# Value products in quarters: riding in the free row tiles of score steps

## The chip, the cores and the metric

The kernel runs on one core of one Trainium2 chip. What counts is the device time of one execution in microseconds (us). The kernel before takes 698.33 us in the median of 3 runs (698.25 to 699.32); the execution that the hardware profiler recorded took 699.02 us, of which 697.3 us lie between its first and its last instruction (the span).

## The reference

Two independent layers over 2048 positions of 640 channels; their outputs stand side by side.

```python
# A: a diagonal state space layer, P = 640 complex states
Lam_bar = exp(dt * Lam);  B_bar = ((Lam_bar - 1) / Lam)[:, None] * Bmat
Bu = einsum("bld,pd->blp", x, B_bar)
h[t] = Lam_bar * h[t-1] + Bu[t]                      # 2048 steps
y = 2 * einsum("blp,dp->bld", h, Cmat).real + x * Dskip
# B: attention, 32 heads of 20, ONE key head and ONE value head for all
q = x @ wq;  k = x @ wk (640 -> 20);  v = x @ wv (640 -> 20)
p = softmax(einsum("bhqd,bkd->bhqk", q, k) * 20**-0.5)
b = einsum("bhqk,bkd->bhqd", p, v) -> (2048, 640) @ wo
```

Inputs and output are bf16. The attention has 32 heads x 2048 x 2048 scores, and their exponentials are most of the work.

## The kernel before

**Tiles.** A score tile is 128 keys x 512 queries of one head. There are 2048 of them (`NTILE`): 4 query blocks x 8 groups of 4 heads x 16 key chunks x 4 heads. 64 successive tiles (4 heads, 16 key chunks) make a block; there are 32 blocks.

**Scores (row tiles).** A score product contracts 20 channels and one row for a bias, so it needs 32 of the 128 rows of TensorE's array. Keys and queries are held four times, at partitions 0, 32, 64 and 96, and up to four products of 32 rows x 128 columns (`tile_position` (32j, 0)) run side by side in one *score step*. `fill` makes a step: two or three tiles for ScalarE, and up to two for VectorE. The results stand in two slots of three PSUM banks, `SC0` and `SC1`; one exp is read out of the one while TensorE fills the other.

**Exponentials.** ScalarE takes two or three tiles in one ACTIVATE (line 1540) and writes bf16 to `PR`. VectorE takes the other tiles: it makes an int16 of a score whose bits are about those of the exponential in bf16 (line 875, to the buffer `BIG`), and shifted copies of it, which GpSimd (line 1913) and VectorE make, correct it in the mean. Each tile of VectorE's so has four value products, on scaled values `VS`, and each of ScalarE's has one, on plain values `VP`.

**Value products (column tiles).** A value product contracts 128 keys to 20 values and a sum, and fills 32 columns of the array. `pv_source` gathers one product of each of the four heads of a block and `pv` issues them as one *column step*, side by side (`tile_position` (0, 32j)), 512 queries each; line 2012. All add up in one PSUM bank, `MB3` (`pvbank`), head j in partitions 32j to 32j + 31. A step may have fewer than four where buffers run short or where the block's products run out. When a block has all its products VectorE copies the bank out (`pvsb`), and the next block's begin.

**The rest of the products** (projections, output projection, state space layer) are written as steps in column tiles too, four quarters of the output columns side by side (`ride` and `product`, line 808). `board` lets such a product *ride*: cut along the contraction into four pieces of 32 rows (`piece`, line 818), each takes a row tile of a score step that the scores leave free. One product at a time may be open, and pieces that found no place are issued alone.

**Order.** All order is made before the launch, by a list scheduler (`Schedule`) with costs of its own: each engine takes the ready instruction with the least priority number, and semaphores follow from the order. `STAGES` holds the rules (priorities, shares, limits) by the number of the score tile reached: SHARE is the part of the tiles that VectorE takes, EV the priority of copies out of PSUM, PV that of value products, BACKLOG and ROOM2 how many copies and free buffers are kept, AHEAD and EARLIER which block VectorE's tiles come from. `background` lists when the other products are due, in score tiles (`CB_FROM`, `Y_STEP`). Engines execute in order and wait for semaphores.

## Time and profile before

| | |
|---|---|
| median of 3 runs | 698.33 us |
| the profiled execution, its span | 699.02 us, 697.3 us |
| TensorE: matmuls, instructions | 683.8 us (98% of the span), 11489 |
| ScalarE | 683.9 us (98%), 705 |
| VectorE | 615.0 us (88%), 1135 |
| GpSimd | 473.1 us (68%), 602 |
| DMA | 34.46 MB, mean 49 GB/s |
| granted TensorE clock | 1.000 |

A matmul's record begins when its data start to stream and ends when its last result is modelled to land, and a record of ScalarE's reaches past the start of the next one. So a busy share near 100% says that an engine was in use, not that it could not have done more: for both, the distance from one start to the next has to be read.

### The profile page before, as it was taken

Reading aid. Unit: us, or ns where it says so; the run is one execution under the profiler, and the core shown is the slowest. Engines: PE = TensorE matmul, PEld = TensorE weight load, DVE = VectorE, ACT = ScalarE, POOL = GpSimd, SP = SyncE. Lnnn points to the kernel's source line nnn. Section 1 sums busy time; section 2 is a strip of 40 time slices with the busy share of each in tenths; the row PEclk is TensorE's granted clock in tenths of the full one; section 3 lists DMA queues with packets and bytes.
Section 4 is the critical chain, followed back from the end, with each engine's and each line's share of the span. In section 5 each row is a group of like instructions: output and inputs, shape, how many; then the busy total and the mean of one; then the engine's idle time right before and its main releaser. Section 6 shows DMA issues by size and latency. Waiting matters only on the chain.

```text
span 697.3 us, 27066 instructions
## 1 busy us (share of the span) xinstructions
PE 683.8 (98%) x11489; PEld 251.2 (36%) x11489; DVE 615.0 (88%) x1135; ACT 683.9 (98%) x705; POOL 473.1 (68%) x602
## 2 busy tenths in 40 slices
PE   9999999999999999999999999999999999999998
PEld 5322232334434433332343332334333332343335
DVE  7899999989888787898988999899999999987885
ACT  7999999999999999999999999999999999999996
POOL 4257756753456686768777887876886788786671
DMA  9659531211210110101111011120000011111001
GB/s 226 169 122 209 137 82 39 61 29 30 78 47 13 31 28 23 40 12 33 40 24 32 19 20 35 45 56 20 12 17 11 21 27 31 27 26 27 22 15 42
DMA packets 81429, 34.46 MB, mean 49 GB/s; under 512 B 62190, under 2 KB 81310, under 8 KB 81310
## 3 DMA queue, kind: packets, MB, share of 16 engines
q1 hardware_dynamic: 80490, 32.57, 19.2%
q8 instruction: 92, 1.51, 0.9%
q10 hardware_dynamic: 820, 0.16, 0.1%
q14 instruction: 27, 0.22, 0.1%
HBM read 11.53 MB, written 9.75 MB: 31 GB/s over the span
## 4 chain that ended last, share of the span: by engine, by line
ACT 49%; PE 48%; SPq 2%; DMA 0%; issue 0%
ACT PR L1540 49%; PE MB L2012 18%; PE MB L808 12%; PE SC L1636 9%; PE MB L818 7%; SPq L723 1%; PE MB L734 1%; DMA wvr<-in_B_wv_dram 0%; PE MB L738 0%; PE SC L734 0%; SPq L719 0%; PE SC L1226 0%; PE MB L1636 0%; ACT PR L2192 0%; SPq L718 0%
## 5 line engine op out<-in xcount | busy, mean ns | idle before, releaser
L1540 ACT ACTIVATE PR<-SC 128x1024 bf16<-128x1024 f32 (+1 forms) x680 | 668.7, 1140 | 4.0 <-PE SC L1636 2.9
L1913 POOL INT64_ADD BIG<-BIG x567 | 460.8, 821 | 198.5 <-DVE BIG L875 53.6
L875 DVE TENSOR_SCALAR BIG<-SC 128x512 int16<-128x512 f32 x562 | 378.7, 685 | 60.0 <-PE SC L1636 53.2
L1636 PE MATMUL SC<-QT,KT 32*128 32x512 bf16 (+1 forms) x2083 | 266.5, 377 | 8.0 <-ACT PR L1540 5.8
L2012 PE MATMUL MB<-BIG,VS 128*32 128x512 bf16 (+1 forms) x2440 | 258.1, 377 | 0.0
L2012 PE MATMUL MB<-PR,VP 128*32 128x512 bf16 (+1 forms) x1502 | 208.0, 378 | 0.0
L1636 PEld LDWEIGHTS SC<-QT,KT 32*128 32x128 bf16 x2083 | 67.3, 91 | 133.3 <-ACT PR L1540 89.5
L2012 PEld LDWEIGHTS MB<-BIG,VS 128*32 128x32 bf16 x2440 | 64.7, 95 | 65.4 <-issue 42.4
L2012 PEld LDWEIGHTS MB<-PR,VP 128*32 128x32 bf16 x1502 | 52.1, 94 | 45.7 <-issue 34.8
L808 PE MATMUL MB<-CA,W 128*32 128x320 bf16 (+2 forms) x984 | 50.9, 299 | 0.3 <-issue 0.3
L808 PE MATMUL MB<-CT,W 128*32 128x512 bf16 (+1 forms) x640 | 35.0, 303 | 0.0
L818 PE MATMUL MB<-xaT,BT 32*128 32x256 bf16 x176 | 34.1, 273 | 0.0
L818 PE MATMUL MB<-diagD,xaT 32*128 32x128 bf16 x320 | 31.4, 217 | 0.1
L808 PE MATMUL MB<-xaT,BA 128*32 128x256 bf16 x800 | 31.2, 274 | 0.0
L818 PEld LDWEIGHTS MB<-diagD,xaT 32*128 32x128 bf16 x320 | 17.7, 92 | 28.5 <-ACT PR L1540 16.6
L808 PEld LDWEIGHTS MB<-CA,W 128*32 128x32 bf16 x984 | 22.7, 96 | 12.4 <-issue 5.6
L808 PE MATMUL MB<-xaT,BT 128*32 128x256 bf16 x624 | 25.6, 274 | 0.0
L870 DVE TENSOR_TENSOR prod<-MB,tab 128x1024 bf16<-128x1024 f32 x20 | 24.3, 1214 | 0.9 <-PE SC L1636 0.9
L2199 DVE CAST stg<-MB 128x512 bf16<-128x512 f32 x35 | 23.7, 678 | 0.7 <-PE MB L818 0.4
L2472 DVE TENSOR_TENSOR_SCAN g<-sc,hst,prod 128x256 bf16<-128x256 f32 x30 | 23.8, 797 | 0.0
L1991 DVE CAST pvsb<-MB 128x512 bf16<-128x512 f32 x31 | 21.2, 682 | 1.2 <-PE MB L2012 1.0
L808 PEld LDWEIGHTS MB<-xaT,BA 128*32 128x32 bf16 x800 | 18.4, 96 | 10.3 <-issue 8.0
(178 smaller groups left out, 512.5 us busy)
## 6 DMA issues: line engine op xcount, KB each, us to landing
out_dram<-stg SPq DMA_DIRECT2D x33, 128.0 KB, 1.8
qd<-BIG SPq DMA_DIRECT2D x20, 128.0 KB, 2.0
QT<-qd SPq DMA_DIRECT2D x28, 80.0 KB
OP<-pvsb SPq DMA_DIRECT2D x105, 20.0 KB
rdP<-recs SPq DMA_DIRECT2D x105, 20.0 KB
lbd<-BA SPq DMA_DIRECT2D x5, 320.0 KB, 3.2
CT<-in_B_x_dram SPq DMA_DIRECT2D x2, 640.0 KB, 5.3
BA<-in_A_B_re_dram SPq DMA_DIRECT2D x1, 800.0 KB, 6.7
```

The lines of the kernel that those rows point to most:

```text
L723: fns = [lambda e, o=o, i=i: e.dma_start_transpose(o, i) for o, i in pairs]
L808: x = e.matmul(out[32 * j:32 * j + 32], lhsT=lhsT[:, 32 * j:32 * j + 32], rhs=rhs, start=start, stop=r.end is tag, tile_position=(0, 32 * ...
L818: return lambda e: e.matmul(out, lhsT=lhsT[at], rhs=rhs[at], start=start, stop=r.end is tag, tile_position=(32 * row, 0), skip_group_check ...
L870: return lambda e: e.tensor_tensor(out, a, b, op)
L875: return lambda e: e.tensor_scalar(out, a, s1, s2, op0=op0, op1=op1)
L1540: ex = self.act(lambda e: e.activation(dst, t[:, 0:512 * n], ACT.Exp, scale=1.0 / UNIT), 0.8333 * 512 * n + 64, table="exp", deps=[op], re ...
L1636: r = e.matmul(out[:, bank.off + lo:bank.off + lo + n], lhsT=p.KT[32 * j:32 * j + 32, 128 * c:128 * c + 128], rhs=p.QT[32 * j:32 * j + 32, ...
L1913: op.fns.append(lambda e: e.int64_add(b.bitcast(I64), a.bitcast(I64), by * 0x0001000100010001))
L1991: ev = self.dve(lambda e: e.tensor_copy(p.pvsb[:, slot, :], bank.ap), 645, deps=[op], reads=[bank.key], writes=[f"pvsb{slot}", f"pvsb{slot ...
L2012: r = e.matmul(bank.tensor[32 * j:32 * j + 32, bank.off + at:bank.off + at + n], lhsT=v[:, c, 0:32], rhs=rhs[:, lo:lo + n], start=first an ...
L2199: ev = self.dve(lambda e: e.tensor_copy(st, bank.ap), 645, deps=[prev], reads=[bank.key], writes=[key], prio=self.EV, gate=(lambda: last.e ...
L2472: o = self.dve(lambda e, ri=ri, init=init: e.tensor_tensor_scan(p.g[:, u, ri, :], rdec, p.prod[:, 1, 0, ri, :], init, ALU.mult, ALU.add), ...
```

## The change

A value product of one of ScalarE's tiles may now ride too. Its 128 keys are cut into four quarters of 32 keys, and each quarter is a product of 32 rows x 128 columns, like a score's, in a row tile that a score step leaves free. Since a row tile writes all 128 partitions of its bank, the 32 columns of values are held between zeros: head j's quarter reads a window of 128 columns in which the values stand at columns 32j to 32j + 31, and adds zeros for the other heads. `ride_values` makes these padded values for key chunks 0 to 7 in four parts of `BIG` that are free once the last queries are projected (4 memsets on GpSimd, 4 DMAs). `pv_board` looks in each score step for a free row tile, before `board` where three row tiles are taken already and a value product is open, and after it in any case. At most one value product is open (`PV_OPEN`); a new one is begun while at least 39 products of the block are outstanding (`PV_LEFT`). `pv_lone` issues left quarters alone at the block's end, and each quarter waits for the one before it (`fence`). Rules and due times are set anew.

```diff
+    VR_N, PVR, PV_OPEN, PV_LEFT = 4, 2, 1, 40
+    def vr(self, kc, j):
+        lo = S * (kc // 2) + S - 384 + 128 * (kc % 2)
+        return self.BIG[:, lo + 96 - 32 * j:lo + 224 - 32 * j]
+    def ride_values(self):
...
+        for r in range(self.VR_N):
+            lo = S * r + S - 384
+            z = self.pool(lambda e, lo=lo: e.memset(p.BIG[:, lo:lo + 384], 0.0), 380, writes=[f"VR{r}"], port=True, prio=0.9)
+            to = p.BIG[:, lo:lo + 256].rearrange("p (c n) -> p c n", c=2)[:, :, 96:128]
+            made.append(self.dma(lambda e, r=r, to=to: e.dma_start(to, p.VP[:, 2 * r:2 * r + 2, :]), 16384, "vr", deps=[z, self.vs_op[r // 2]],
...
+    def pv_board(self, op, used):
+        s, b = self.s, self.pv_b
+        rows = [x for x in range(4) if x not in used]
+        if s.mode == "S" or not rows or not self.PVR or not self.vr_op or self.pv_rode is op:
+            return
+        best = next(((o, x) for o in self.pv_open for x in rows if x in o[2]), None)
+        if best is None:
...
+            for j in sorted(range(4), key=lambda j: -len(self.pvq[b][j])):
+                can = [e for e in self.pvq[b][j] if e[6] == "VP" and e[1] < 2 * self.VR_N and e[4].end is not None and s.seen(e[4], "pe") <= s.t]
...
+            self.pvq[b][j] = [x for x in self.pvq[b][j] if x is not can[-1]]
+            best = [can[-1], j, {0, 1, 2, 3}], rows[0]
+            self.pv_open.append(best[0])
+        self.pv_ride(op, *best)
+        used.add(best[1])
+    def pv_ride(self, op, o, x, stop=False):
+        (_, kc, rhs, key, _, h, _), j, left = o
+        w, bank, at = self.vr(kc, j), self.pvbank, slice(32 * x, 32 * x + 32)
+        op.fns.insert(0, lambda e: e.matmul(bank.ap, lhsT=w[at], rhs=rhs[at], start=False, stop=stop, tile_position=(32 * x, 0),
+                                            skip_group_check=True))
...
+        if self.pv_rode is not None and (op.fence is None or op.fence.start < self.pv_rode.start):
+            op.fence = self.pv_rode
...
@@ fill
+        if self.PVR > 2 or self.PVR > 1 and self.pv_open or not self.rides or len(used) < 3:
+            self.pv_board(op, used)
         self.board(op, used)
+        self.pv_board(op, used)
@@ STAGES, CB_FROM, Y_STEP (a few of the values)
-            'COPY1': 0.792, 'P1OWN': 0.391, 'PVEV': 0.2, 'SCARCE': 8, 'BACKLOG': 9, 'GRACE': 55.439, 'SHARE': 0.281, 'MISC_FIRST': 0,
+            'COPY1': 0.792, 'P1OWN': 0.391, 'PVEV': 0.2, 'SCARCE': 8, 'BACKLOG': 10, 'GRACE': 55.439, 'SHARE': 0.281,
...
-        (850, {'STAY': 1.2, 'PAUSE': 1035.401, 'dve': 179.397, 'PATIENCE': 2500.0, 'MARGIN': 765.584, 'WAITING': 2, 'REFILL': 766.143,
+        (935, {'STAY': 1.2, 'PAUSE': 1035.401, 'dve': 179.397, 'PATIENCE': 2500.0, 'MARGIN': 765.584, 'WAITING': 2, 'REFILL': 766.143,
...
-    CB_FROM, CB_STEP = 172.381, 9.233
+    CB_FROM, CB_STEP = 102.641, 9.233
```

No share of VectorE's is changed in the rules, but the new order comes out with other counts. Those that differ, counted in the order of the whole program (a value product on `VP` or `VS` is 128 rows x 32 columns, on 512 queries, or on 256 in the last block):

| instructions | before | after |
|---|---|---|
| ScalarE, exp of 2 tiles (128x1024) | 581 | 577 |
| ScalarE, exp of 3 tiles (128x1536) | 98 | 103 |
| ScalarE, exp of 1 tile (128x512) | 1 | 0 |
| VectorE, first step of a tile | 591 | 585 |
| value products on `VP`, of 512 and of 256 | 1412, 90 | 1375, 94 |
| value products on `VS`, of 512 and of 256 | 2288, 152 | 2272, 136 |
| quarters of value products in row tiles | 0 | 164 |
| score steps with all four row tiles in use | 359 | 466 |
| other products as pieces in row tiles (line 818 before, 819 now) | 708 | 616 |
| fillers that keep the array warm, `KT,VZ` of 256 | 160 | 172 |

The first place is on TensorE at score tiles 855 to 866, in a unit of the state space layer (`xaT` with `BA` and `BT`). A row is so many matmuls of a kind; line 1636 is a score, 808 a column step's quarter, 818 a piece in a row tile. Before:

```order
L1636 MATMUL SC<-QT,KT 128x512 x3
L808 MATMUL MB<-xaT,BA 32x256 x20
L818 MATMUL MB<-xaT,BT 128x256
L1636 MATMUL SC<-QT,KT 128x512 x3
L818 MATMUL MB<-xaT,BT 128x256
L808 MATMUL MB<-xaT,BA 32x256 x16
L818 MATMUL MB<-xaT,BT 128x256
L1636 MATMUL SC<-QT,KT 128x512 x3
```

Now (line numbers are those of the new file: 1705 a score, 809 a column step's quarter, 870 a quarter of a value product):

```order
L1705 MATMUL SC<-QT,KT 128x512 x3
L809 MATMUL MB<-xaT,BA 32x256 x20
L870 MATMUL MB<-PR,BIG 128x512
L1705 MATMUL SC<-QT,KT 128x512 x3
L809 MATMUL MB<-xaT,BA 32x256 x20
L809 MATMUL MB<-xaT,BT 32x256 x8
L870 MATMUL MB<-PR,BIG 128x512
L1705 MATMUL SC<-QT,KT 128x512 x3
```

The fourth row tile of these score steps held pieces of the unit; it now holds quarters of a value product, and the unit's products stand in column steps.

The second place is on TensorE at the end of a block, score tiles 906 to 915: the last column steps of value products before VectorE copies the bank out. Before:

```order
L1636 MATMUL SC<-QT,KT 128x512 x3
L2012 MATMUL MB<-BIG,VS 32x512 x2
L2012 MATMUL MB<-PR,VP 32x512 x4
L2012 MATMUL MB<-BIG,VS 32x512 x2
L1636 MATMUL SC<-QT,KT 128x512 x3
```

Now (line 2100 is a value product in a column tile):

```order
L1705 MATMUL SC<-QT,KT 128x512 x3
L2100 MATMUL MB<-BIG,VS 32x512 x3
L2100 MATMUL MB<-PR,VP 32x512
L2100 MATMUL MB<-BIG,VS 32x512 x6
L2100 MATMUL MB<-PR,VP 32x512
L2100 MATMUL MB<-BIG,VS 32x512
L1705 MATMUL SC<-QT,KT 128x512 x3
L2100 MATMUL MB<-PR,VP 32x512
L809 MATMUL MB<-xaT,BA 32x256 x4
```

The block used to end in a step of four products; now one product is left over and makes a column step by itself.

The third place is ScalarE's last exps (line 1540 before, 1609 now), and the copy that follows them. Before:

```order
L1540 ACTIVATE PR<-SC1 128x1024
L1540 ACTIVATE PR<-SC0 128x1536
L1540 ACTIVATE PR<-SC1 128x1536
L1540 ACTIVATE PR<-SC0 128x1536
L1540 ACTIVATE PR<-SC1 128x512
L1997 ACTIVATE pvsb<-MB3 128x256
```

Now:

```order
L1609 ACTIVATE PR<-SC1 128x1024
L1609 ACTIVATE PR<-SC0 128x1536
L1609 ACTIVATE PR<-SC1 128x1536
L1609 ACTIVATE PR<-SC0 128x1536
L1609 ACTIVATE PR<-SC1 128x1536
L2085 ACTIVATE pvsb<-MB3 128x256
```

The last exp, for which the last value products and all that follows wait, has three tiles in place of one.

63 lines of the change are left out of this document (52 added, 11 removed).

## The prediction

> **What bounds the kernel now.** I read the page's shares first, then the groups by shape, then ScalarE's and TensorE's rows in order of time, last the waits.
>
> ```profile
> PE 683.8 (98%) x11489; PEld 251.2 (36%) x11489; DVE 615.0 (88%) x1135; ACT 683.9 (98%) x705; POOL 473.1 (68%) x602
> L1540 ACT ACTIVATE PR<-SC 128x1024 bf16<-128x1024 f32 x581 | 546.7, 1076 | 3.4 <-PE SC L1636 2.2 <-PE MB L2012 0.6
> L1540 ACT ACTIVATE PR<-SC 128x1536 bf16<-128x1536 f32 x98 | 141.6, 1521 | 0.7 <-PE SC L1636 0.7
> ```
>
> TensorE and ScalarE both look full, and the exps show 4 us of idle time. But one exp of two tiles is recorded for 1.08 us while 581 of them cover 546.7, 0.94 each: the records overlap, and a short wait hides in the overlap. So I take distances from start to start. Two answers for ScalarE each give a pair of rows; the last exp of the first row is the first exp of the second, or the one before the last is:
>
> ```profile
> 606.53 11.11 ACT L1540 ACTIVATE PR<-SC 128x1024 bf16<-128x1024 f32 x12 [0.18 <-PE MB L2012]
> 616.49 2.07 ACT L1540 ACTIVATE PR<-SC 128x1024 bf16<-128x1024 f32 x2
> 135.36 8.16 ACT L1540 ACTIVATE PR<-SC 128x1536 bf16<-128x1536 f32 x6
> 140.68 2.84 ACT L1540 ACTIVATE PR<-SC 128x1536 bf16<-128x1536 f32 x2
> 18.09 1.02 ACT L1540 ACTIVATE PR<-SC 128x1024 bf16<-128x1024 f32 x1 [1.50 <-PE SC L1636]
> 688.66 0.67 ACT L1540 ACTIVATE PR<-SC 128x512 bf16<-128x512 f32 x1
> ```
>
> The twelfth exp of the first row starts at 616.49: 11 distances of 9.96 / 11 = 0.905 us. The fifth of the third row starts at 140.68: 4 distances of 1.330. So a third tile costs 0.425, and an exp of one tile would take 0.48. First and last exp start at 18.09 and 688.66, 670.6 apart. The exps before the last need 581 x 0.905 + 98 x 1.330 = 656.2. So ScalarE loses 14.4 us to waits in the whole run: it is within 2.1% of its own limit.
>
> TensorE, over three score steps:
>
> ```profile
> 607.72 0.39 PE L818 MATMUL MB<-CA,W 32*128 32x512 bf16 x1
> 607.72 0.39 PE L1636 MATMUL SC<-QT,KT 32*128 32x512 bf16 x3
> 608.04 0.39 PE L2012 MATMUL MB<-PR,VP 128*32 128x512 bf16 x1
> ...
> 615.86 0.39 PE L1636 MATMUL SC<-QT,KT 32*128 32x512 bf16 x3
> 616.18 0.39 PE L2012 MATMUL MB<-PR,VP 128*32 128x512 bf16 x1
> ...
> 616.41 0.38 PE L2012 MATMUL MB<-BIG,VS 128*32 128x512 bf16 x1
> ...
> 616.63 0.39 PE L2012 MATMUL MB<-PR,VP 128*32 128x512 bf16 x3
> ...
> 616.95 0.39 PE L1636 MATMUL SC<-QT,KT 32*128 32x512 bf16 x3
> 617.27 0.40 PE L2012 MATMUL MB<-BIG,VS 128*32 128x512 bf16 x4
> 617.50 0.38 PE L2012 MATMUL MB<-PR,VP 128*32 128x512 bf16 x1
> ...
> 617.82 0.39 PE L1636 MATMUL SC<-QT,KT 32*128 32x512 bf16 x3
> ```
>
> A column step follows another after 0.22 us (616.18, 616.41, 616.63). From a score step to the first column step, and from the last column step to a score step, it takes 0.32: a change between row and column tiles costs about 0.10 beyond a step's 0.22. So a score step with two column steps takes 0.87 (616.95 to 617.82), with three 1.09 (615.86 to 616.95), while an exp of two tiles takes 0.905. With these prices on each step of the order, TensorE needs 655 us from the second score fill to the last, ScalarE 654 for the exps in it, and 669.6 pass. The two engines are equal in load; each holds up the other by turns, since with two slots neither gets further ahead than about one exp.
>
> ```profile
> PEld SC L1636 <- ACT PR L1540: 89.5, 216, 0.8
> DVE BIG L875 <- PE SC L1636: 53.2, 173, 1.9
> ACT PR L1540 <- PE SC L1636: 2.9, 6, 1.5
> ```
>
> The waits say the same: weight loads of scores wait for exps (89.5 us, while streams still run), VectorE waits for scores, and of ScalarE's waits only the longest show. VectorE (88%) and GpSimd (68%) follow.
>
> **The change, part by part.** I price each part against the profiled execution (699.02; span 697.3) and carry the difference to the median, 698.33.
>
> *ScalarE.* 577 x 0.905 + 103 x 1.330 against 581 x 0.905 + 98 x 1.330 + 0.48: -3.6 + 6.65 - 0.48 = **+2.6 us**. There are six more tiles on ScalarE, and as many instructions. Of this 0.85 us is the last exp alone (1.33 for 0.48), and that part is on the end's path whatever happens before:
>
> ```profile
> 687.65 0.39 PE L1636 MATMUL SC<-QT,KT 32*128 32x256 bf16 x2
> ...
> 689.42 0.42 PE L2012 MATMUL MB<-PR,VP 128*32 128x256 bf16 x6
> ...
> 689.88 0.39 ACT L1997 ACTIVATE pvsb<-MB 128x256 bf16<-128x256 f32 x1 [0.54 <-PE MB L2012]
> ```
>
> The last value products start at 689.42, just when the exp of 688.66 has ended (689.33), and ScalarE's copy waits for them. What follows them has the same products in both orders.
>
> *TensorE, value products.* 41 ScalarE tiles' products go to the 164 quarters; with six more tiles on ScalarE and six fewer on VectorE, 53 products of 512 and 12 of 256 leave the column steps: 53/4 + 12/8 = 14.75 steps of 512, at 0.22 **-3.2 us**. But a block ends when one head has a product fewer than the others: before, all column steps of a block hold four products (0.75 of a step is unfilled in the whole program), now in 29 places a step at a block's end holds one to three, 12.5 steps' worth unfilled: **+2.6 us**.
>
> *TensorE, the others.* The quarters take rows that other products had: 92 pieces less ride, and these products (state space, output projection, the skip products) come back as column steps, 10.6 steps of 512: **+2.3 us**. 12 more fillers are 1.5 steps, **+0.3**. Row-mode work grows by 5.4 steps of 512, left quarters and pieces issued alone, at 0.21 **+1.1**, and six more changes between the modes at 0.10 are **+0.6**. The sum for TensorE: -3.2 + 2.6 + 2.3 + 0.3 + 1.1 + 0.6 = **+3.7 us**. So the engine that was to be relieved has more to do.
>
> *A quarter itself.* A piece in the fourth row tile costs nothing that the rows show: the score step at 607.72 with it takes 0.32 to the first column step, as that at 615.86 without. The bound above is its weight load, if it were not hidden:
>
> ```profile
> L1636 PEld LDWEIGHTS SC<-QT,KT 32*128 32x128 bf16 x2083 | 67.3, 91 | 133.3 <-ACT PR L1540 89.5 <-DVE BIG L875 23.8 <-issue 12.9
> ```
>
> 107 more score steps are full; 107 x 0.091 = 9.7 us. Below zero it can't go: nothing is taken from a step that it joins. I take 0, the row of the same thing. The Trainium skill (TensorE: Matmul & The Clock Gate, Part 3, The mechanism) says that a weight load overlaps running matmuls only where the row group differs, and that packed tiles start about 4 ns apart; by the first a step that fills all four row groups leaves its next load no free one, by the second the 107 cost 0.4 us. The trace's pair at 607.72 and 615.86 agrees with the second.
>
> *Fences.* Each quarter waits for the score step of the one before it, 0.87 us earlier or more, which has landed (0.39 after its start). Nothing. Two in direct succession, a left quarter issued alone behind a step with a quarter, wait some 0.2 each: at most one a block, inside the +1.1 or, at worst, 29 x 0.2 = 6 us. I take 0 beyond the sum; 6 goes to the range's upper end.
>
> *GpSimd, SP.* Four memsets of 128x384 by the row of 128x512 take 0.5 each at most:
>
> ```profile
> L1022 POOL MEMSET QT<- 128x512 bf16 x10 | 5.2, 524 | 6.8 <-DVE M L874 4.8 <-DVE VS L870 1.4
> L1913 POOL INT64_ADD BIG<-BIG x567 | 460.8, 821 | 198.5 <-DVE BIG L875 53.6 <-DVE g L2472 21.9 <-PE MB L2012 12.3
> ```
>
> They stand once between GpSimd's adds, which wait 198.5 us in all: hidden; without that cover 2 us, once. Five adds fewer (4 us of GpSimd) gain nothing for the same reason. The four DMAs stand in SP's queue behind a block's `rdP` and ahead of the next block's `sums`; SP is held until the memsets end, and that block's normalised rows come later by as much, for an output product that is due tens of tiles later. Nothing, or 2 us once without that cover.
>
> *VectorE.* Six first steps fewer, some 4 us of 615; it waits 53.2 us for scores, so what it saves becomes wait.
>
> *Due times and rules.* The tasks at `CB_FROM` begin 70 tiles earlier, and TensorE's load there rises from 38.0 to 38.9 us in exps 41 to 80, where ScalarE's is 41.3: hidden.
>
> **The sum.** Both engines get more, but not their sum. I cut both orders into stretches of a fixed number of exps and take in each the larger of TensorE's and ScalarE's need. Stretches of 40: 662.2 before, 665.4 after, +3.2. Stretches of 8: 669.5 before, which is what was measured (669.6), and 671.4 after, **+1.9**. I take the latter, since it gives the time of before without a rest, and add the last exp, **+0.85**: +2.7 us (4.0 with the former). On the median: 698.33 + 2.7 = **701.0 us**; this profiled execution would have been 701.8.
>
> **Rivals.**
>
> *Faster: ScalarE's waits shrink.* Of ScalarE's 14.4 us of waits much comes from three column steps between two scores (1.09 against 0.905). Such runs fall from 138 to 120; if each cost its 0.185 that would be -3.3 us. Against it, runs of four steps (1.30) rise from 55 to 62, +2.8, and of two and a half (0.98) from 55 to 66, +0.8; with the rest the sum is about -1. Decides from: waits down by over 4.0, which pays the 2.6 and 1.4 (0.2% of the median, about what a measurement of this kernel can tell from no change). The order of the steps, not their count, would do it: a score step that is issued just as its slot comes free covers a long run behind it. With 5.5 less: 695.4. I see no row for it, but the trace shows the waits to be there, and a new order can hit them either way: 0.17.
>
> *No change that can be measured.* The same, with waits down by 1.2 to 4.0, or +2.6 of exps of which the run-length sum returns 1 and shorter evacuations the rest: 698.8. 0.27.
>
> *Slower by far: the quarters stall TensorE.* The 9.7 us of weight loads, or 6 at the fences, or both in part: 705 to 710, say 706. The Trainium skill (TensorEngine Tiling, Restrictions and Gotchas) says that different row tiles can't access one PSUM bank at the same time and that software must keep them apart; here all quarters go to `MB3`, one in a step, fenced. The pieces that ride before are of that kind already and show no stall. 0.05.
>
> **Chances.** The forecast (slower by 1.4 to 5 us): 0.51, centred on 701.0, of its own 699.8 to 703.3. With the rivals: faster by over 0.2% 0.17, within 0.2% 0.27, slower 0.56. The range leaves out half of the faster rival below 697.0 and the slow one above 703.7.
>
> **What would show it.** Right: exps of two and three tiles again 0.905 and 1.33 apart in runs; the first to last exp some 672 to 673 apart instead of 670.6; score steps with a quarter still 0.32 from the next column step; a value step of one to three products at block ends; the last exp 1.33. Wrong: first to last exp under 669, which would mean that the waits fell by more than the exps grew; or score steps with a quarter longer than 0.32; or waits of TensorE on its own semaphore at the quarters.

## The result, and the profile after

The changed kernel takes 705.37 us in the median of 4 runs (704.87 to 706.48), the one before 698.83 (698.25 to 700.01): a ratio of 1.0094, 95% interval 1.0074 to 1.0113. It is slower by 6.5 us. The prediction said slower, by 2.7 (701.0, range 697.0 to 703.7): the side is right, the size is wrong, and the time lies outside the range.

The profiled execution took 705.62 us (span 703.5; before 699.02 and 697.3). The page's shares, the exps by shape, and the waits (who waits for whom: us in all, times, longest):

```profile
PE 687.1 (98%) x11600; PEld 251.1 (36%) x11600; DVE 613.8 (87%) x1125; ACT 686.7 (98%) x705; POOL 474.3 (67%) x601
L1609 ACT ACTIVATE PR<-SC 128x1024 bf16<-128x1024 f32 x577 | 543.5, 1074 | 6.8 <-PE SC L1705 5.7 <-PE MB L2100 0.6 <-PE MB L1705 0.2
L1609 ACT ACTIVATE PR<-SC 128x1536 bf16<-128x1536 f32 x103 | 148.2, 1533 | 1.2 <-PE MB L870 0.7 <-PE MB L2100 0.3
PEld SC L1705 <- ACT PR L1609: 61.6, 147, 0.9
DVE BIG L939 <- PE SC L1705: 58.4, 182, 2.4
DVE BIG L938 <- DMA qd<-BIG: 2.5, 2, 1.8
```

The shares say nothing: both engines are as full as before. The idle time of the exps says more, 6.8 and 1.2 us where before showed 3.4 and 0.7, and two new names stand in it: L870, a quarter, and a wait of VectorE for the transfer `qd`. ScalarE's rows in order of time, by first and last exp and the four longest waits between:

```profile
18.06 1.02 ACT L1609 ACTIVATE PR<-SC 128x1024 bf16<-128x1024 f32 x1 [1.46 <-PE SC L1705]
...
89.43 1.02 ACT L1609 ACTIVATE PR<-SC 128x1024 bf16<-128x1024 f32 x1 [1.35 <-PE SC L1705]
...
239.81 2.01 ACT L1609 ACTIVATE PR<-SC 128x1024 bf16<-128x1024 f32 x2 [1.02 <-PE SC L1705]
...
326.86 1.45 ACT L1609 ACTIVATE PR<-SC 128x1536 bf16<-128x1536 f32 x1 [0.74 <-PE MB L870]
...
486.57 2.44 ACT L1609 ACTIVATE PR<-SC 128x1024 bf16<-128x1024 f32 x2 [0.98 <-PE SC L1705]
...
693.20 2.84 ACT L1609 ACTIVATE PR<-SC 128x1536 bf16<-128x1536 f32 x2
```

The last exp starts at 693.20 + 1.33 = 694.53, so first and last are 676.5 apart; before it was 670.6. With the prediction's prices (0.905 for an exp of two tiles, 1.330 for three) every distance from exp to exp splits into what the exp needs and a wait. I sort the waits at 0.15 us, which is less than one step of TensorE. The same for all kernels of this study, each from its own trace:

| kernel | first exp | exps need | waits over 0.15 (number) | waits up to 0.15 | from last exp's start to the end | time, median | ratio to before, 95% interval |
|---|---|---|---|---|---|---|---|
| before | 18.09 | 656.1 | 5.4 (18) | 9.1 | 8.6 | 698.83 | |
| after | 18.06 | 657.8 | 9.7 (19) | 8.9 | 9.0 | 705.37 | 1.0094, 1.0074 to 1.0113 |
| e1 abs later | 18.18 | 657.8 | 8.7 (20) | 9.3 | 9.0 | 705.16 | 1.0083, 1.0068 to 1.0097 |
| e2 no lone | 18.06 | 657.8 | 7.9 (19) | 9.2 | 9.0 | 704.53 | 1.0071, 1.0059 to 1.0083 |
| e3 shift after | 22.73 | 657.8 | 8.1 (18) | 8.7 | 9.0 | 709.93 | 1.0152, 1.0139 to 1.0165 |
| e4 all three | 23.01 | 657.8 | 9.9 (21) | 8.6 | 9.0 | 709.72 | 1.0149, 1.0131 to 1.0167 |
| e5 transpose later | 18.18 | 657.8 | 7.6 (16) | 9.0 | 9.0 | 704.03 | 1.0084, 1.0058 to 1.0109 |
| e6 shift 128 | 18.66 | 657.8 | 6.3 (18) | 9.1 | 9.1 | 703.23 | 1.0056, 1.0044 to 1.0068 |
| e7 combined | 18.66 | 657.8 | 5.2 (16) | 9.1 | 9.3 | 702.37 | 1.0045, 1.0033 to 1.0057 |
| e8 no rides | 18.92 | 662.5 | 9.2 (23) | 7.9 | 13.4 | 711.65 | 1.0183, 1.0165 to 1.0201 |
| e9 rides, old rules | 18.86 | 657.5 | 10.9 (25) | 9.0 | 8.8 | 707.56 | 1.0107, 1.0081 to 1.0133 |
| e10 shift before | 20.10 | 656.1 | 5.4 (18) | 9.2 | 8.8 | 701.66 | 1.0030, 1.0014 to 1.0046 |
| e11 ROOM2 back | 18.31 | 659.2 | 8.3 (24) | 8.6 | 8.6 | 705.05 | 1.0087, 1.0074 to 1.0100 |
| e12 repaired | 19.08 | 657.8 | 6.4 (18) | 8.8 | 9.0 | 703.56 | 1.0067, 1.0052 to 1.0082 |

After against before: exps +1.7, short waits -0.1, long waits +4.3, the end +0.4, and a first exp that starts 0.03 earlier: within their rounding, the 6.2 us of the span. The short waits, in which the two engines hold up each other by turns, are the same. The long ones are a handful of stops: 1.47 us at 87 to 89, 1.30 at 238 to 240, 1.12 at 485 to 487 and 0.86 at 326 make 4.75, where before had a single one over 0.4 (0.94 us at 481). Here is what stands behind each.

*The stop at 88 us.* SP's queue, VectorE, TensorE of the changed kernel:

```profile
80.61 3.23 SPq L724 DMA_TRANSPOSE BA<-lbd  x1
84.30 0.83 SPq L1394 DMA_DIRECT2D qd<-BIG  x1
...
88.03 0.29 DVE L938 TENSOR_SCALAR BIG<-BIG 128x512 int16<-128x512 int16 x1 [1.81 <-DMA qd<-BIG]
...
88.98 0.38 PE L819 MATMUL MB<-BIG 32*128 32x512 bf16 x1 [1.21 <-DVE BIG L939]
```

SP issues the transpose for 3.23 us, and `qd`, which copies a projected query block out, comes only behind it. It then takes 3.70 us to land, where the `qd` transfers issued at 80.12 and 89.59 took 1.8 each. VectorE's absolute value overwrites that block in place, so it waits for the copy, 1.81 us, and behind it stand the first steps of VectorE's score tiles. TensorE's next score step waits for the first of these, and ScalarE, whose next exp reads that step, waits 1.35. No quarter has been issued by then; the first starts at 158.3 us.

*The standstills of TensorE.* At 238.92 and 485.81 in the changed kernel, and at 482.02 in the kernel before (last two rows), the row names no releaser but "issue":

```profile
237.51 0.23 PE L809 MATMUL MB<-CT,W 128*32 128x128 bf16 x4
237.57 0.23 PE L809 MATMUL MB<-CA,W 128*32 128x128 bf16 x4
238.92 0.24 PE L809 MATMUL MB<-CT,W 128*32 128x128 bf16 x4 [1.12 <-issue]
...
484.66 0.23 PE L809 MATMUL MB<-BIG,xaT 128*32 128x128 bf16 x3
485.81 0.38 PE L809 MATMUL MB<-BIG,xaT 128*32 128x128 bf16 x13 [0.93 <-issue]
```

```profile
480.69 0.51 PE L808 MATMUL MB<-BIG,xaT 128*32 128x128 bf16 x24
481.13 0.39 PE L1636 MATMUL SC<-QT,KT 32*128 32x512 bf16 x1
482.02 0.39 PE L1636 MATMUL SC<-QT,KT 32*128 32x512 bf16 x2 [0.50 <-issue]
```

All three fall into a run of short products of 128 columns, four every 0.06 us, and one stops TensorE in the middle of a score step, with one product of three issued.

*The quarters that are left alone.* At 325.5 a score step with a quarter in it is followed by two left quarters:

```profile
325.52 0.39 PE L870 MATMUL MB<-PR,BIG 32*128 32x512 bf16 x1
325.53 0.39 PE L1705 MATMUL SC<-QT,KT 32*128 32x512 bf16 x3
325.99 0.09 PEld L870 LDWEIGHTS MB<-PR,BIG 32*128 32x128 bf16 x1 [0.37 <-PE SC L1705]
326.43 0.09 PEld L870 LDWEIGHTS MB<-PR,BIG 32*128 32x128 bf16 x1 [0.35 <-PE MB L870]
```

Each waits until the one before it has landed: 0.47 and 0.44 us from start to start, not 0.21. They read the tile of `PR` that the next exp writes, so the exp of 326.86 waits for them. Of the 164 quarters three stand alone; the others ride, and a score step with one still takes 0.32 to the next column step (0.325 in the mean over the 154 such steps that a column step follows; with a piece in the fourth row tile it was 0.325 in the mean over 165 steps of the kernel before):

```profile
239.37 0.39 PE L870 MATMUL MB<-PR,BIG 32*128 32x512 bf16 x1
239.37 0.39 PE L1705 MATMUL SC<-QT,KT 32*128 32x512 bf16 x3
239.69 0.39 PE L2100 MATMUL MB<-PR,VP 128*32 128x512 bf16 x1
```

### The profile page after: what moved, and what is told of

Its sections match the earlier page's. It is cut to its first block, busy times and chain, and to the rows that moved or that the text cites. A ratio compares the mean times of both kernels' runs of the same rounds, so it can differ in the third digit from the quotient of the medians.

```text
span 703.5 us, 27301 instructions
## 1 busy us (share of the span) xinstructions
PE 687.1 (98%) x11600; PEld 251.1 (36%) x11600; DVE 613.8 (87%) x1125; ACT 686.7 (98%) x705; POOL 474.3 (67%) x601
## 3 DMA queue, kind: packets, MB, share of 16 engines
q8 instruction: 93, 1.52, 0.9%
## 4 chain that ended last, share of the span: by engine, by line
PE 64%; ACT 31%; SPq 2%; DMA 1%; DVE 1%; issue 1%
ACT PR L1609 31%; PE MB L2100 24%; PE MB L809 17%; PE SC L1705 8%; PE MB L819 7%; PE MB L870 6%; SPq L724 2%; PE MB L739 1%; PE SC L735 1%; DMA qd<-BIG 1%; DMA wvr<-in_B_wv_dram 0%; DVE BIG L939 0%; PE MB L735 0%; PE MB L1705 0%; SPq L1444 0%
## 5 line engine op out<-in xcount | busy, mean ns | idle before, releaser
L2100 PE MATMUL MB<-BIG,VS 128*32 128x512 bf16 (+1 forms) x2408 | 261.3, 377 | 0.5 <-DVE pvsb L2079 0.2
L2100 PE MATMUL MB<-PR,VP 128*32 128x512 bf16 (+1 forms) x1469 | 213.6, 377 | 0.2 <-DVE pvsb L2079 0.2
L2100 PEld LDWEIGHTS MB<-BIG,VS 128*32 128x32 bf16 x2408 | 67.0, 95 | 65.3 <-issue 40.2
L2100 PEld LDWEIGHTS MB<-PR,VP 128*32 128x32 bf16 x1469 | 55.1, 94 | 44.5 <-issue 30.0
L870 PE MATMUL MB<-PR,BIG 32*128 32x512 bf16 x164 | 63.0, 384 | 0.5
L809 PE MATMUL MB<-CA,W 128*32 128x320 bf16 (+2 forms) x1012 | 53.4, 300 | 0.1
L870 PEld LDWEIGHTS MB<-PR,BIG 32*128 32x128 bf16 x164 | 14.9, 91 | 56.5 <-ACT PR L1609 34.7
L819 PE MATMUL MB<-diagD,xaT 32*128 32x128 bf16 x288 | 28.2, 217 | 0.0
L819 PEld LDWEIGHTS MB<-diagD,xaT 32*128 32x128 bf16 x288 | 15.9, 92 | 27.7 <-ACT PR L1609 17.8
```

The lines of the kernel that those rows point to most:

```text
L809: x = e.matmul(out[32 * j:32 * j + 32], lhsT=lhsT[:, 32 * j:32 * j + 32], rhs=rhs, start=start, stop=r.end is tag, tile_position=(0, 32 * ...
L819: return lambda e: e.matmul(out, lhsT=lhsT[at], rhs=rhs[at], start=start, stop=r.end is tag, tile_position=(32 * row, 0), skip_group_check ...
L870: op.fns.insert(0, lambda e: e.matmul(bank.ap, lhsT=w[at], rhs=rhs[at], start=False, stop=stop, tile_position=(32 * x, 0), skip_group_chec ...
L2100: r = e.matmul(bank.tensor[32 * j:32 * j + 32, bank.off + at:bank.off + at + n], lhsT=v[:, c, 0:32], rhs=rhs[:, lo:lo + n], start=first an ...
```

## Experiments

Theory 1 throughout: the 3.8 us that the prediction missed are a few stops, each with a cause of its own (from profile to profile it is 3.5 us: 6.2 of span against 2.7). Theory 2: TensorE simply has more work than I had counted, and a stop that is taken away comes back elsewhere. Where a kernel differs by a few lines, they stand where the finished order (`o`, or `plan.s.order`) is handed to the emitter, so every other instruction keeps its place; line numbers in those kernels' rows are some lines higher.

**The stop at 88 us.** First I moved VectorE's instruction (e1), then the transfer ahead of it (e5).

```diff
+ # e1: the absolute value of QP1 behind the next two VectorE steps
+ x = o.pop(k); o.insert(o.index(late) + 1, x)
```

> The changed kernel with one instruction moved on VectorE: the in-place absolute value that waited 1.81 us for its block's qd transfer at 88.03 us now stands two instructions later, behind the two BIG<-SC steps that stood behind it. All else is as in the changed kernel (705.4 us). Theory 1 (the lost time is a few single stops): the 1.35 us wait of ScalarE at 89.4 us falls below 0.4 us and the time by 1.0 to 1.4, to 704.0 to 704.4. Theory 2 (TensorE has more work than before and any wait taken away comes back as another a little later): the wait goes, but the time stays within 0.4 of 705.4.

705.16 us. The wait at 88 is gone (0.22 us on VectorE), but little is gained, 1.0 us of long waits, and 0.53 of that is a shorter standstill at 239, which no edit touched. GpSimd's next add waits for the moved instruction (3.69 us; it had waited 4.34), and part of the delay comes back through GpSimd's adds at 93.6 (ScalarE then waits 0.50 and 0.18). Another instruction of the same kind waits for its own `qd` in this trace, at 71.8, and costs ScalarE 0.82; it stands ahead of everything that the edit moved, so the edit is not what made it wait:

```profile
71.84 0.29 DVE L943 TENSOR_SCALAR BIG<-BIG 128x512 int16<-128x512 int16 x1 [1.06 <-DMA qd<-BIG]
...
93.64 0.69 DVE L944 TENSOR_SCALAR BIG<-SC 128x512 int16<-128x512 f32 x1 [1.01 <-POOL BIG L1987]
```

So moving the instruction took the stop at 88 away (1.75 us of ScalarE's waits) and brought 0.68 back. Theory 2's time came out, but by named waits, one of which the edit did not make. Whether the transfer itself can come in time is the next run's question.

```diff
+ # e5: the transpose BA<-lbd behind the transfer qd<-BIG on SP's queue
+ o.remove(x)                       # x: the transfer "ba1"
+ o.insert(index_of_qd1 + 1, x)
```

> The changed kernel with one transfer moved on SP's queue: the transpose BA<-lbd, whose issue held SP for 3.23 us from 80.61 us, stands behind the transfer qd<-BIG that had to wait for it until 84.30; VectorE's and every other engine's order is that of the changed kernel. Theory 1 (the stop at 88 us comes from SP's queue, not from the place of the absolute value): qd lands by about 86, VectorE's 1.81 us wait for it falls below 0.3, ScalarE's 1.35 us at 89.4 with it, and the time falls by 1.0 to 1.5 from 705.4, to 703.9 to 704.4; GpSimd, which stood 4.34 us behind that instruction, runs earlier too, so that nothing comes back as it did when the instruction itself was moved. Theory 2 (the transfer takes 3.7 us wherever it is issued): the wait stays over 1 us and the time within 0.4 of 705.4.

704.03 us, as expected. SP issues the transfer ahead of the transpose, VectorE does not wait there, and ScalarE runs sixteen exps in one row where the stop was:

```profile
79.95 1.85 SPq L1398 DMA_DIRECT2D qd<-BIG  x2
82.26 3.52 SPq L728 DMA_TRANSPOSE BA<-lbd  x1
...
85.95 0.28 DVE L942 TENSOR_SCALAR BIG<-BIG 128x512 int16<-128x512 int16 x1
...
79.30 16.61 ACT L1613 ACTIVATE PR<-SC 128x1024 bf16<-128x1024 f32 x16
```

Long waits fall by 2.2, first to last exp by 2.0. The runs spread over 703.2 to 709.0, so the ratio's interval doesn't separate it from the changed kernel's; the trace does.

**The quarters that stand alone** (e2). They are left out, and with them their part of three value products: this kernel does less work.

```diff
+ o[:] = [x for x in o if not (x.eng == "pe" and len(x.fns) == 1 and x.reads[0][:2] == "VR")]
```

> The changed kernel without the three quarters that are issued alone (at 325.99, 326.44 and 465.51 us); their share of three value products is left out, nothing else changes. Theory 1 (single stops): ScalarE's wait of 0.74 us at 326.9 us falls below 0.15 us, and the time from 705.4 by 0.6 to 0.9, to 704.5 to 704.8. Theory 2 (TensorE's work as a whole): 705.2 to 705.4, since 0.65 us of row-mode work less is a thousandth of the work. A third theory, that the fences of all 164 quarters cost, would leave 705.0 or more too, and a sum of waits for fences elsewhere that this kernel keeps.

704.53 us: 0.84 less, and the long waits fell by 1.9, of which 0.86 is the stop at 326 (0.19 is left nearby) and 0.75 a shorter standstill at 238, which no edit touched. The intervals overlap with the changed kernel's; the size of the fall is what theory 1 said for this stop, and the stop is gone from the trace.

**The standstills** (e3, e6, e10). If TensorE's instructions come in packets, a standstill must sit on a grid: at one of the places in the count of instructions, one packet apart, where a new packet begins. I call these places the grid's lines. And a standstill must leave its products when instructions are put ahead of the program. The page's row for the queue that carries them (packets, MB, share):

```profile
q8 instruction: 93, 1.52, 0.9%
```

1.52 MB in 93 packets are 16 KB each, and 11600 products, 11600 weight loads and 629 semaphore instructions are 23829 recorded TensorE instructions, 256 for each packet. Counted from the program's start, 7361 recorded TensorE instructions stand ahead of the standstill at 238.9, 16065 ahead of that at 485.8, and 16065 and 11457 ahead of those at 482.0 and 353.0 (0.5 us) of the kernel before. All four numbers are a multiple of 256 plus 193. (A few records can be missing from a trace, so such a count may come out two or three low.)

```diff
+ tiny = plan.mm(plan.pvbank.cols(0, 16), plan.PR[:, 0, 0:128], plan.PR[:, 0, 0:16], True, True)
+ warm.fns[:] = [tiny] * N + warm.fns      # e3: N 66, two fillers out; e6: 16; e10 (before): 26
```

> The changed kernel with 66 products of 16 columns, on zeros, put before the first of the start's filler products, and two later fillers taken out: 128 TensorE instructions more ahead of everything, and the order of all else as it was. Theory 1 (TensorE's instructions arrive in packets of 256, and a stretch that uses up a packet in less than about 3.4 us stands still until the next has come): where the packets end moves 128 instructions earlier, the two standstills of 1.34 us at 237.6 and 1.14 us at 484.7 that no instruction is named for fall below 0.5 each, ScalarE's waits of 1.30 and 1.12 us there go with them, and the time falls by 1.3 to 2.2, to 703.2 to 704.1, unless a standstill arises elsewhere. Theory 2 (the standstills belong to the products themselves, a weight or an operand that is late): both stay where they are in the program, with 1.1 to 1.4 us each, and the time at 705.2 to 705.6.

709.93 us. Here I had miscounted: the program writes each of these products as four of 32 columns, so 520 instructions came on top, 2 x 256 + 8, and the grid moved by 8 only. The standstills stayed, with 7873 and 16577 instructions ahead of them, which is again 193 above a multiple of 256; they did not stay with their products, which would have had 7881 and 16585. And the edit made a standstill of its own, where no operand can be late, since all these products have the same operands:

```profile
1.25 2.01 PE L739 MATMUL MB<-PR 128*32 128x16 bf16 x223 [1.25 <-DVE PR L1049]
7.22 0.48 PE L739 MATMUL MB<-PR 128*32 128x16 bf16 x41 [3.96 <-issue]
```

223 products with their loads run in 2.01 us, then TensorE stands still for 3.96, when 449 recorded instructions are done: 256 + 193. The first exp comes 4.67 us later than in the changed kernel. The median is 4.6 us slower; the profiled execution only 2.9, as 1.8 us less pass from first to last exp, 0.8 of them because ScalarE waits 0.64 at the stop that took 1.47.

> The changed kernel with 16 products of 128x16 (each four of 32 columns) on zeros before the first filler of the start: 128 TensorE instructions more, which is half of a packet of 256 and too few to use one up at the start; all else in its order. Theory 1 (every standstill of TensorE sits at one place in a grid of 256 instructions, where a packet was used up in less than 3.4 to 3.9 us): the standstills at 237.6 (1.34 us) and 484.7 (1.14 us) fall below 0.4 each, as the grid's line now falls 128 instructions earlier into a looser stretch; ScalarE's waits there, 1.30 and 1.12, fall below 0.4; the time falls by 1.2 to 2.0, to 703.4 to 704.2. Theory 2 (they belong to the products): they stay at 1.1 to 1.4 us and the time at 705.2 to 705.7.

703.23 us, and its interval, 1.0044 to 1.0068, lies below the changed kernel's. The grid's line now falls 128 instructions earlier into the first run; there and at the next line, 7617, this is left:

```profile
238.54 0.24 PE L812 MATMUL MB<-BIG,xaT 128*32 128x128 bf16 x4
238.98 0.24 PE L812 MATMUL MB<-BIG,xaT 128*32 128x128 bf16 x4 [0.20 <-issue]
...
240.03 1.94 ACT L1612 ACTIVATE PR<-SC 128x1024 bf16<-128x1024 f32 x2 [0.23 <-PE SC L1708]
```

At 485 the standstill moved to the line 16321 and is 0.75 us long, more than the 0.4 I expected, but ScalarE's waits there are 0.25 and 0.32 instead of 1.12. The stop at 88 us is not in this trace (VectorE waits 0.6 us in two for `qd`), though SP's order is that of the changed kernel: `qd`, issued at 84.70, landed 2.39 us later instead of 3.70. Why it was quicker is open; the edit was not aimed at it. So of the 3.3 us between first and last exp that this kernel gained, 1.8 are that stop, which is luck, and 1.4 the standstills. The standstills are also not equally long from run to run: ScalarE's waits at the two places add up to 1.5 to 2.4 us in the changed kernel and in e1 to e5, whose grid did not move or moved by 8, and to 1.0 to 1.1 in e6, e7 and e12, whose grid moved by 128.

> The kernel before with 26 products of 128x16 (each four of 32 columns) on zeros ahead of the first filler: 208 TensorE instructions more, nothing else. Theory 1 (the grid of 256 instructions): its standstill of 0.89 us at 481.1 us, in which ScalarE waited 0.94, falls below 0.4, the time by 0.4 to 0.8 from 699.2, to 698.4 to 698.8, or as much slower where the grid's lines now fall into another dense stretch (226, 350, 412 or 622 us). Theory 2 (the standstill belongs to its products): it stays at 0.9 us, the time at 699.0 to 699.5.

701.66 us; the first exp is 2.0 us later, and from there to the last it takes 670.8 as against 670.6. The standstill at 481 is gone, and the one at 353 (0.5 us) has become this:

```profile
355.05 0.45 PE L811 MATMUL MB<-BIG,xaT 128*32 128x128 bf16 x20
356.34 0.35 PE L811 MATMUL MB<-BIG,xaT 128*32 128x128 bf16 x12 [0.84 <-issue]
```

It is theory 1's second half: the line left one dense run for another. The price at the start I had not expected.

That the supply is what runs dry is shown by the grid, by e3, and by the packets themselves, since the traces hold the time of each: there are as many as lines of the grid, one after each. In the changed kernel one lands at 237.41, TensorE reaches its line at 237.58 and goes on at 238.91. In e3 one lands at 5.93, and TensorE, which has stood still since 3.09, goes on at 7.22. Over the 14 traces there are 32 standstills over 0.35 us at a line for which the trace names no releaser; at each of them TensorE goes on 1.2 to 1.6 us after the packet has landed, and no line of any trace is passed sooner than 1.1 us after its packet. So the length of a standstill hangs on when the packet lands as well as on the products: before the same products at the same line it was 1.34 us in the changed kernel and in e5, 0.80 in e1 and 0.59 in e2.

The runs before the three standstills shown above used up their 256 instructions in 2.6 to 2.9 us, and the lines came 3.5 to 4.0 us apart, the standstill included. That is no threshold: in e8 a line was passed without a stop 2.8 us after the one before (241.46), as its packet had landed 1.5 us earlier; and in the changed kernel TensorE stood still for 0.41 us until 566.32, though 5.5 us had passed since the line before, as the packet landed only at 564.93. The Trainium skill (Runtime: NRT & Kernel Launch, Instruction fetch mechanics) says that instructions come in blocks of 16 KiB, 256 of them, fetched while the block before is executed, and calls the cost of a boundary mostly hidden. The block's size is that of the grid here; the cost is not hidden where short products with their weight loads follow each other without a pause.

**All at once** (e4, e7, e12). e4 has the edits of e1, e2 and e3; e7 those of e5, e2 and e6; e12 those of e5 and e6, with all work done.

> The changed kernel with all three edits: the absolute value two instructions later, no quarter issued alone, 128 TensorE instructions ahead. Theory 1 (single stops, each worth its wait): 705.4 less 1.0 to 1.4, 0.6 to 0.9 and 1.3 to 2.2 is 700.9 to 702.5, which is the sum of the prediction (701.0) within its own uncertainty; ScalarE's waits over 0.15 us add up to about 5.5 us where the changed kernel has 9.7 and the one before 5.4. Theory 2 (TensorE's work): 704.5 or more, with the waits spread anew over the same blocks.

709.72 us, since two of its three edits were the wrong ones: it has the late start of e3 (23.01), and four waits of 0.5 to 1.2 us at 91 to 100 us, where the moved absolute value waits 1.03 us for `qd` once more and GpSimd 4.49 us for the absolute value.

> The changed kernel with the transfer moved, the three quarters that stand alone left out, and 128 TensorE instructions ahead. Theory 1 (single stops, each worth its wait): 705.4 less 1.0 to 1.5, 0.84 (measured for the lone quarters) and 1.2 to 2.0 is 701.1 to 702.4, the prediction's 701.0 within its working; first to last exp 672.3 to 673.5 us where the prediction had 672.4 and the changed kernel has 676.5. Theory 2 (TensorE's work as a whole is what was mis-sized): 703.5 or more, ScalarE's waits spread over other places.

702.37 us, and first to last exp are 672.07 us apart:

```profile
18.66 1.94 ACT L1617 ACTIVATE PR<-SC 128x1024 bf16<-128x1024 f32 x2 [1.46 <-PE SC L1713]
...
689.40 2.84 ACT L1617 ACTIVATE PR<-SC 128x1536 bf16<-128x1536 f32 x2
```

(689.40 + 1.33 - 18.66.) The long waits are at 5.2, where the kernel before has 5.4, with the changed kernel's exps, its order and all its quarters but the three left out. Theory 1's figures came out: the time at their upper edge, the distance 0.2 below its lower one. What is left against before is 1.7 of exps, 0.7 at the end, 0.6 at the start (the instructions put ahead, at least in part) and -0.2 of waits.

> The changed kernel, nothing left out, with the transfer BA<-lbd behind qd<-BIG and 128 TensorE instructions ahead of the start. Theory 1 (single stops): e7's 702.4 and 0.84 for the lone quarters, so 702.9 to 703.4, which is what e6 had without the transfer moved, as the stop at 88 us was not there in its trace either; waits over 0.15 us about 6.2 us. Theory 2 (gains add up run by run, 1.3 of e5 and 2.1 of e6): 701.6 to 702.2.

703.56 us, 0.2 above theory 1's figures and 1.4 above theory 2's. The gains of e5 and e6 do not add up, because e6 had lost the stop at 88 already. This kernel, which leaves nothing out, is still slower than before by 0.52 to 0.82%; nothing here beats the kernel before.

**The rules and the quarters apart** (e8, e9, e11).

```diff
- 'PVR': 2,      # e8: no quarters
+ 'PVR': 0,
```

> The changed kernel's rules and due times without any quarter (PVR 0): 680 exps, 564 of two tiles, 115 of three and 1 of one, so 4.2 us more of exp time than the changed kernel (663.9 against 659.7 by 0.905, 1.330 and 0.48). Theory 1 (the new rules, not the quarters, cost the time): 2 to 5 us over the changed kernel's 705.4 from the exps alone if waits stay, so 705 to 710, and slower than before by 1 to 1.6%. Theory 2 (the quarters cost it, by their fences and weights): near the kernel before, 698 to 701. Its trace tells which waits it shares with the changed kernel: the one at 88 us should be there, since no quarter rides so early.

711.65 us: far from theory 2's 698 to 701, and above theory 1's 710. (The count of 680 took the last output copy for an exp; there are 679.) Under these rules more tiles go to ScalarE without quarters, +4.6 us, VectorE waits for `qd` as long as with them (longest 1.9 us), and 13.4 us of other work are left behind the last exp instead of 9.0. So the new rules, not the quarters, bring the stop at 88, and they are no good without quarters.

In e9 the tables `STAGES`, `CB_FROM` and `Y_STEP` are those of the kernel before, with the four numbers for quarters added.

> The quarters under the rules of the kernel before: its table of rules, CB_FROM 172.381 and Y_STEP 33.854, with PVR 2, PV_OPEN 1, PV_LEFT 39, PV_DRAIN 9; 188 quarters, 681 exps or so (581 of two tiles, 100 of three, 1 of one, so 2.2 us more of exp time than before by 0.905, 1.330 and 0.48). Theory 1 (the quarters cost nothing by themselves, and the time of the changed kernel lies in stops that its order happens to have): 699.2 plus 1 to 3, so 700 to 702.5, with no 1.8 us wait for qd at 88 us, since up to the last block's projections the order is that of before. Theory 2 (the quarters cost, by fences, weights or mode changes): 703 or more under these rules too. Theory 3 (they are worth what they take off TensorE): 699 or less.

707.56 us; theory 2's time. There is no stop at 88 (VectorE waits 0.4 for `qd`), and the short waits are again 9.0; but the long waits are 10.9 us:

```profile
317.25 1.02 ACT L1608 ACTIVATE PR<-SC 128x1024 bf16<-128x1024 f32 x1 [1.20 <-PE MB L2099]
...
486.86 1.94 ACT L1608 ACTIVATE PR<-SC 128x1024 bf16<-128x1024 f32 x2 [1.32 <-PE SC L1704]
```

The first is an exp that waits for value products, the readers of its place in `PR`; the second is a standstill of 1.36 us on the grid's line; and four quarters stand alone. Theory 1 of this run falls in its number: I had taken the order of before to be free of stops once the quarters are added, and it is not. ScalarE's waits for quarters that stand alone are 1.2 us of it (0.66 at 426.8, 0.50 at 654.0). So each half of the change alone costs more than both together: the quarters 8.2 us (707.56 against 699.37), the rules 12.4 (711.65 against 699.23), both 6.5. These two runs change the whole order, so they do not give a price of the quarters as such.

```diff
- 'ROOM2': 2,    # e11
+ 'ROOM2': 1,
```

> The changed kernel with one number of its rules as before: ROOM2 1 in place of 2. It is the only number of the first stage that moves a step before 100 us (with CB_FROM, EV, BACKLOG, AHEAD or the PV of the third stage put back alone, every engine's order stays that of the changed kernel). 581 exps of two tiles, 101 of three and 1 of one, which is 1.0 us more of exp time than the changed kernel by 0.905, 1.330 and 0.48; 189 rows with quarters in place of some 160. Theory 1 (the stop at 88 us is this number's): no wait of VectorE for qd over 0.5 us, and ScalarE's waits in exps 40 to 80 fall from 2.44 us to below 1.0, the kernel before having 0.68; the rest of the order is new, so the time may be 703 to 708, with the sum of the waits below 0.15 us at 9.5 to 10.6 as in every kernel so far, and the waits above it what decides. Theory 2 (the quarters or their copies bring that stop): it stays.

705.05 us. The stop at 88 is gone: VectorE's only wait for `qd` is 0.5, and exps 40 to 80 lose 0.6 us to waits, as before. So it is `ROOM2` that put the transpose and `qd` into that place. The gain is spent: 1.4 us more of exps, and six quarters that stand alone, three of them in a row, for which an exp waits:

```profile
425.50 1.27 PE L870 MATMUL MB<-PR,BIG 32*128 32x512 bf16 x3
...
426.81 1.94 ACT L1609 ACTIVATE PR<-SC 128x1024 bf16<-128x1024 f32 x2 [0.94 <-PE MB L870]
```

## Why the prediction was right, and where it was wrong

The side was right, and partly for the reasons given: with the three stops below cured or left out, e7 is still 0.33 to 0.57% slower, mostly by terms that the sum had (the exps and the end; 0.6 us of a later start are not among them). The size was wrong because the sum added loads and took three things at nothing: the new order of the transfers ("hidden", 1.75 us), the quarters that stand alone ("0 beyond the sum", 0.86) and the standstills (no term, 1.5 more than before). That is 4.1 us; the last exp, taken 0.5 too large, and the short waits leave the 3.5 that the prediction missed from profile to profile.

- *ScalarE, +2.6 with 0.85 of it the last exp.* 1.7 us more up to the last exp is what the trace has (657.8 against 656.1, where the prediction rounded to 656.2). The last exp is one of three tiles as predicted, but from its start to the end only 0.36 us came on top, not 0.85 (0.7 in e7). This term was too large by 0.5; why the end takes up so much of it was not traced.
- *TensorE, +3.7, mostly hidden behind the exps.* Nothing speaks against it, though no run measures the 3.7 itself. The sum over stretches of 8 exps had +1.9 from first to last exp; with the new stops gone it is 672.07 - 670.57 = +1.5 (e7, which leaves three quarters out), and 1.7 of exps alone make that. Short waits stayed within 0.3 us of before's in every kernel, or below.
- *A quarter itself, 0.* Right for those that ride: 0.32 us from a score step with a quarter to the next column step, in 154 steps. The 9.7 us of weight loads, the upper bound, did not come.
- *Fences, 0 beyond the sum.* Wrong. I had "some 0.2 each" for quarters in direct succession, inside the +1.1. They cost 0.24 beyond a step each, but what I left out is that their tile of `PR` is the one that the next exp writes: the wait went to ScalarE in full, 0.86 us. In e2's trace it is gone; the 0.84 by which e2's median is lower agrees with it, but lies within the overlap of the two intervals. Waits of TensorE on its own semaphore at the quarters were one of the signs of being wrong that the prediction had named.
- *Due times and rules, "hidden".* The largest error. I looked at TensorE's load in exps 41 to 80, and that is indeed below ScalarE's, but a load says nothing on the order within it. The stop at 88 us costs 1.75 with the 0.28 before it. I even named the wrong number: with `CB_FROM` alone put back, every engine's order is the same; with `ROOM2` back (e11) the stop is gone. How late `qd` lands depends on more than the order, as e6 shows. SP's queue I looked at for the four new transfers only, not for those that the rules moved.
- *Standstills.* No step of the prediction had them, though the row of before at 482.02 was there to be read: 0.94 us of ScalarE's waits came from it. In the changed kernel 2.42 us did, which is 1.5 more, by where the grid's lines fall and, from run to run, by when the packets land (in e2 it was 1.59).
- *The sum by stretches.* That the stretches of 8 gave the 669.6 us that had passed made me trust it. It was no reason to: the sum has no term for a wait on a transfer, a fence or the instruction supply, so it gave the right total with 1.3 us of standstills in it (0.94 at 482 and 0.37 at 354) that it did not know of. The other sixteen of before's waits over 0.15 us, 4.1 us in all, have no standstill ahead of them (TensorE's products start at most 0.34 us apart there); they may be load that the sum did price.
- *The rivals.* "Slower by far" (705 to 710, at 0.05) holds the time, but its mechanism, quarters that stall TensorE by weight loads or fences, made 0.86 us of it. The faster one, with fewer waits, had the right place, ScalarE's waits, and the wrong sign. That the time fell into the range of the first is no merit of its price.

Not settled is why every order of this study with quarters or with the new rules ends above before; e7 puts 1.7 us of it down to tiles that VectorE no longer takes, but why VectorE takes fewer was not tried.

## What to carry to other kernels

Where two engines are equally full, as here, a sum of loads gave the part that hardly changed, and the reordering was paid in single stops. So look in the new order for three things: a transfer issued behind a long transpose whose buffer is overwritten by an instruction with others behind it, a product left for the end whose buffer the next writer waits for, and runs of short products long enough to use up the instruction supply. Sort the waits by length before they are summed: here those up to 0.15 us stayed the same, and the four over 0.8 each had a cause of their own; those between were not all followed. And before a stop is cured by moving the instruction that waits, look who waits for that one (in e1 0.68 us came back through GpSimd). One trace is not enough for the size of such a stop: the one at 88 us and the standstills came out shorter in runs whose edits did not touch them.

## What the runs showed of the hardware

- TensorE's instructions come in packets of 16 KB, 256 recorded instructions each. At the lines between them, 193 above a multiple of 256, it stood still until 1.2 to 1.6 us after the packet had landed: 0.4 to 1.4 us within the program, 3.96 us after 223 products of 16 columns at the very start. The profile shows such a wait as "issue" where it names anything, and it can fall into the middle of a score step.
- A transfer of one kind does not always take the same time: `qd` behind a transpose landed 3.70 us after its issue in the changed kernel and 2.39 in e6, with the same order on SP's queue, and others took 1.8.
- Instructions put ahead of the program are not free: 208 made the first exp 2.0 us late (e10), 520 made it 4.7 late (e3). With 128 it was 0.6 to 1.0 late (e6, e7, e12), but first exps 0.8 late were seen without any (e8, e9), so their price is not shown.
- Row products into one bank that wait for each other take 0.44 to 0.47 us from start to start, where steps that don't take 0.22.
